# Second pass of the second MoE: activation steps of three blocks by turns, two sets of PSUM banks, stores from ScalarE's queue

## The chip, the cores and the metric

The program runs on one core of a Trainium2 chip. The metric is the device time of one execution in microseconds. A time given for a kernel is the median of several runs; a profile is one execution recorded by the hardware profiler, and its span runs from the first to the last instruction.

## What is computed

Three stages follow one another: a chunked attention, a first mixture of experts with a skip score, and a second stage that the reference calls MoE 2. Only the last one is touched. Its input is a matrix x of 4608 tokens by 512; `w_in` is 512 by 2048 and `w_out` 2048 by 512.

```python
def _moe2_ref(x, w_in, w_out):
    h = x @ w_in
    beta = 1.0
    neg = h <= -beta
    pos = h >= beta
    g = np.where(pos, h, np.where(neg, 0.0, (h + beta) ** 2 / (4.0 * beta)))
    return (g @ w_out).astype(np.float32)
```

## The kernel before, in words

The second stage cuts the 4608 tokens into 9 groups (`NG`) of 512 tokens (`GT`), and the 2048 hidden columns into 16 blocks (`NF`) of 128. A block (g, m) is a tile of 128 hidden columns by 512 tokens; there are 144 of them, in the order of the list `seq`. The stage runs in two passes over this list.

The first pass (`s_A`, L1147 and on) makes a block of h with 12 matmuls into a PSUM tile `a`, copies it on ScalarE to a tile `hs` (L1155) and stores it to a tensor `h_dram` from ScalarE's own queue (L1156).

The second pass reads each block back with `load_h` (L1158), a DMA of 256 KB from SyncE's queue into one of 8 buffers `hs` (`NH`). Then `s_G` computes the activation in six steps that take turns between ScalarE (ACT) and VectorE (DVE): Relu on ACT (L1167), maximum and subtraction on DVE (L1168), Square on ACT (L1169), the sum on DVE (L1170), the cast to the rounded half `gh` on ACT (L1171) and the remainder `gl` on DVE (L1172). Each step reads what the step before it wrote. The profile shows the tile that holds h as `hs`, the temporary as `r`, and `gh`, `gl` as `xh`, `xl` (they lie in the buffers `xh1`, `xl1`, four blocks deep, picked by `n % KD`). `w_out` is held as two halves too, `bh` and `bl` in the profile.

`s_B` multiplies the block: for each of the four token quarters t, three matmuls (gh by the high half, gh by the low half, gl by the high half) add to the PSUM tile `b0` to `b3`. So a block is 12 matmuls of 128 by 512, and the third one of the first quarter is the first that reads `gl`. At a group's last block (m = 15) each quarter's sum is copied out to a tile `o` (tag `s`, two buffers): t = 0 and 2 on ACT (L1188), 1 and 3 on DVE (L1186), and stored from SyncE's queue (L1190).

The order is written out by hand, and each engine follows its own instructions in the order of the program. In the loop at the end of `tile_attn_moe_kernel`, turn n runs `s_G` for block n, then `load_h` for block n + 6, then `s_B` for block n - 2 (`LAG` is 2).

Of the kernel before, what the change touches and what calls it, by code (L numbers as in the profile page):

```python
# [7 lines left out]
F32 = mybir.dt.float32  # L8
# [7 lines left out]
PSUM = bass.MemoryType.PSUM  # L16
# [3 lines left out]
NT, DM = B * S, H * D  # L20
NE, F1, F2 = 8, 1024, 2048
P = 128
CH = 64
KD = DM // P
# [9 lines left out]
NF = F2 // P  # L34
# [52 lines left out]
def kernel(ctx, tc, q, k, v, w_skip, w_gate, w1, w2, w_in, w_out, consts, out):  # L87
    nc = tc.nc
# [8 lines left out]
    dec_p = ctx.enter_context(tc.tile_pool(name="dec", bufs=2))  # L97
# [38 lines left out]
    def mm(o, l, r, start=True, stop=True):  # L136
        nc.tensor.matmul(out=o, lhsT=l, rhs=r, start=start, stop=stop)  # L137
# [80 lines left out]
    def settle():  # L218
        while done:
            next(done.pop(0), None)  # L220
# [72 lines left out]
    def warm(n, b=None):  # L293

        for _ in range(n):
            mm((big() if b is None else b)[:, 0:512], ones_b, cb[:, 0:512])
# [144 lines left out]
    def s_SEL(*us):  # L441

        if us[0] < 0:
            return []
        b = bank()
        for n, u in enumerate(us):
            ls = T.pop(("ls", u))
            for s in range(2):
                mm(b[:, 32 * n + 16 * s:32 * n + 16 * s + 16], ls[:, s * P:s * P + P], cst[:, 0:16])
        return e_SEL(us, b)  # L450
# [200 lines left out]
    xg_t, xt_t, h_t = {}, {}, {}  # L651
# [150 lines left out]
    with tc.manual_schedule():  # L802
# [44 lines left out]
        for i in range(NU - 1):  # L847
# [28 lines left out]
            a, r = s_SEL(i - 2), s_RANK(i - 3)  # L876
# [17 lines left out]
        b = s_SEL(u - 2)  # L894
# [19 lines left out]
        b = s_SEL(u - 1, u)  # L914
# [6 lines left out]
        w = s_RANK(u - 1, u)  # L921
# [17 lines left out]
        for s in range(4):  # L939
# [3 lines left out]
            out=key, in0=cnt, scalar=float(NE), in1=cst[:, C_PREF - C_SEL:C_PREF - C_SEL + NE], op0=ALU.mult, op1=ALU.add  # L943
# [7 lines left out]
            out=perm, in0=cst[r24, C_POS - C_SEL:C_POS - C_SEL + NL], scalar=own[r24, 1:2], in1=cst[r24, C_BLK - C_SEL:C_BLK - C_SEL + NL], op0=ALU.is_equal, op1=ALU.mult  # L951
# [42 lines left out]
    with tc.If(total > 0):  # L994
        fb = tc.tile_pool(name="fb", bufs=1, reuse_waits="tile")
        with fb as f_p, tc.For_i(0, NE, 1) as j:
# [4 lines left out]
            with tc.For_i(0, n_j, 1) as b:  # L1001
# [8 lines left out]
                    out=fx, out_offset=None, in_=x_dram[:, :], in_offset=bass.IndirectOffsetOnAxis(ap=fi[:, 0:1], axis=0)  # L1010
# [5 lines left out]
                for h in range(4):  # L1016
                    w = f_p.tile([P, KD, 2 * P], F32, tag="fw", name="fw", bufs=3)
                    nc.sync.dma_start(
                        out=w, in_=w1.rearrange("e (k p) f -> p (e k) f", p=P)[:, bass.ds(e * KD, KD), h * 2 * P:(h + 1) * 2 * P]
# [7 lines left out]
                for h in range(4):  # L1027
                    w = f_p.tile([P, 2, DM], F32, tag="fw", name="fw", bufs=3)
                    nc.sync.dma_start(
                        out=w, in_=w2.rearrange("e (f p) d -> p (e f) d", p=P)[:, bass.ds(e * (F1 // P) + 2 * h, 2), :]  # L1030
                    )
                    for a in range(2):
                        f = 2 * h + a
                        mm(bk, fh[:, f, :], w[:, a], f == 0, f == F1 // P - 1)
                nc.vector.scalar_tensor_tensor(
                    out=fx[:, 0:DM], in0=bk, scalar=fx[:, GATE:GATE + 1], in1=fx[:, 0:DM], op0=ALU.mult, op1=ALU.add
                )
                nc.gpsimd.indirect_dma_start(
                    out=x_dram[:, :],
                    out_offset=bass.IndirectOffsetOnAxis(ap=fi[:, 0:1], axis=0),  # L1040
                    in_=fx,
# [5 lines left out]
    xs_t, GT = {}, 512  # L1047
# [61 lines left out]


    ps_moe.close()
    p2 = ctx.enter_context(tc.tile_pool(name="p2", bufs=1, space=PSUM, reuse_waits="tile"))
    NG = NT // GT
    LAG = 2
    NH = 8
    x2_t, g_t, b_t, h_t = {}, [], {}, {}

    def t_X2(g, h, src, tag="t"):
        b = p2.tile([P, 512], F32, tag=tag, name=tag, bufs=2 if tag == "t" else 1)
        for kk in range(KD):  # L1120
            tr(b[:, kk * P:kk * P + P], src[:, kk * P:kk * P + P])
        return b

    def e_X2(g, h, a, b):
        if g not in x2_t:
            x2_t[g] = [x2_p.tile([P, KD, GT], F32R, tag=nm, name=nm, bufs=1) for nm in (f"xh{g % 2}", f"xl{g % 2}")]
        xh, xl = x2_t[g]
        b3 = b.rearrange("p (k n) -> p k n", k=KD)
        cut = slice((2 * h + a) * P, (2 * h + a + 1) * P)
        nc.scalar.copy(out=xh[:, :, cut], in_=b3)  # L1130
        nc.vector.tensor_tensor(out=xl[:, :, cut], in0=b3, in1=xh[:, :, cut], op=ALU.subtract)  # L1131

    def s_X2(g, h, tag="t"):
        bs = [t_X2(g, h, src, tag if tag == "t" else f"b{a}") for a, src in enumerate(xs_t.pop((g, h)))]
        return lambda: [e_X2(g, h, a, b) for a, b in enumerate(bs)]

    def mm_A(b, g, m, cut):
        xh, xl = x2_t[g]
        o = m % 8 * P
        for kk in range(KD):  # L1140
            wh, wl = (w[:, o:o + P] for w in w_t["in", kk * 2 + m // 8])
            for n, (w, x) in enumerate(((wh, xh), (wh, xl), (wl, xh))):
                mm(b[:, cut], w, x[:, kk, cut], kk == 0 and n == 0, kk == KD - 1 and n == 2)
# [14 lines left out]
    def load_h(g, m):  # L1158
        h_t[g, m] = g_p.tile([P, GT], F32, tag="hs", name="hs", bufs=NH)
        nc.sync.dma_start(out=h_t[g, m], in_=h_dram[g][m])  # L1160

    def s_G(n, g, m):

        h = h_t.pop((g, m))
        r = dec_p.tile([P, GT], F32, tag="a", name="r")
        gh, gl = (t[:, n % KD] for t in g_t)
        nc.scalar.activation(out=r, in_=h, func=ACTF.Relu, bias=bias[:, 0:1])  # L1167
        nc.vector.scalar_tensor_tensor(out=h, in0=h, scalar=-1.0, in1=r, op0=ALU.max, op1=ALU.subtract)  # L1168
        nc.scalar.activation(out=h, in_=h, func=ACTF.Square, scale=0.5, bias=bias[:, 1:2])  # L1169
        nc.vector.tensor_tensor(out=r, in0=r, in1=h, op=ALU.add)  # L1170
        nc.scalar.copy(out=gh, in_=r)  # L1171
        nc.vector.tensor_tensor(out=gl, in0=r, in1=gh, op=ALU.subtract)  # L1172

    def s_B(n, g, m):
        gh, gl = (t[:, n % KD] for t in g_t)
        wh, wl = (w[:, m % 2 * 512:m % 2 * 512 + 512] for w in w_t["out", m // 2])
        for t in range(4):
            if m == 0:
                b_t[t] = p2.tile([P, DM], F32, tag=f"b{t}", name=f"b{t}")
            cut = slice(t * P, t * P + P)  # L1180
            for n, (h, w) in enumerate(((gh, wh), (gh, wl), (gl, wh))):
                mm(b_t[t], h[:, cut], w, m == 0 and n == 0, m == NF - 1 and n == 2)
            if m == NF - 1:
                o = dec_p.tile([P, DM], F32, tag="s", name="o")
                if t % 2:
                    nc.vector.tensor_copy(o, b_t[t])  # L1186
                else:
                    nc.scalar.copy(out=o, in_=b_t[t])  # L1188
                r0 = g * GT + t * P
                nc.sync.dma_start(out=out[r0:r0 + P, :], in_=o)  # L1190

    a_t = {}
    with tc.manual_schedule():
        b = t_X2(0, 0, xs_t[0, 0][0])
        moe.close()
        x2_p = ctx.enter_context(tc.tile_pool(name="x2", bufs=2, reuse_waits="tile"))
        g_p = ctx.enter_context(tc.tile_pool(name="g", bufs=2, reuse_waits="tile"))
        e_X2(0, 0, 0, b)
        spare = p2.tile([P, DM], F32, tag="b3", name="spare")
        warm(8, spare)  # L1200
        e_X2(0, 0, 1, t_X2(0, 0, xs_t[0, 0][1]))
        warm(4, spare)
        load_x(0, 1)
        settle()
        for m in range(4):
            tag = "aatt"[m]
            a_t[0, m] = p2.tile([P, GT], F32, tag=tag, name=tag, bufs=2)
            if m == 3:
                rest = s_X2(0, 1, "b")
            mm_A(a_t[0, m], 0, m, slice(0, 2 * P))  # L1210
        rest()
        for m in range(4):
            mm_A(a_t[0, m], 0, m, slice(2 * P, GT))
        seq = [(g, m) for g in range(NG) for m in range(NF)]
        settle()
        for n, (g, m) in enumerate(seq):
            s_A(g, m)
            if n < KD:
                load_kept(KD + n)
            if n >= 8 and n % 6 == 0:  # L1220
                step()
            if n == len(seq) - 8:
                g_t.extend(x2_p.tile([P, KD, GT], F32R, tag=nm, name=nm, bufs=1) for nm in ("xh1", "xl1"))
            if n >= len(seq) - 8:
                load_h(*seq[n - len(seq) + 8])
            if n >= len(seq) - LAG:
                s_G(n - len(seq) + LAG, *seq[n - len(seq) + LAG])
            if g + 1 < NG:
                if m in (2, 6):
                    load_x(g + 1, m // 6)  # L1230
                if m in (8, 12):
                    s_X2(g + 1, m // 12)()
        settle()
        for n in range(LAG, len(seq) + LAG):
            if n < len(seq):
                s_G(n, *seq[n])
            if n + NH - 2 < len(seq):
                load_h(*seq[n + NH - 2])
            s_B(n - LAG, *seq[n - LAG])


# [22 lines left out]
```

## Time and profile before

| | us |
|---|---|
| median of 3 runs | 1481.36 (1478.95 to 1491.36) |
| the profiled execution's own time | 1479.77 |
| its span, first to last instruction | 1478.0 |

The profiled execution's time is 1.77 us longer than its span; sums over the trace are set against its own time, 1479.77, which is 1.6 us under the median. Over the span TensorE (PE) is busy 1329.7 us, VectorE 696.3, ScalarE 663.4 and GpSimd 214.1. A busy matmul here is counted to its modelled end and overlaps the next one, so PE's speed is read from the starts of its matmuls. The granted clock is a share: 1.00 is 2.4 GHz and 0.50 is 1.2 GHz. In the timeline a row gives the start, the duration, the engine, the line and operation, and in brackets how long the engine sat idle before it and what ended that.

### The profile page before, as it was taken

What the parts mean: (1) busy time and instruction counts of PE and PEld (TensorE: products, weight loads), DVE (VectorE), ACT (ScalarE), POOL (GpSimd) and SP (SyncE); (2) the same over time, 40 slices, a digit from 0 to 9 for tenths busy, and PEclk for the clock granted to TensorE, in tenths of its full rate; (3) what the DMA queues carried; (4) which work ended last, traced back from release to release, by engine and by line L of the source; (5) the groups of instructions that cost most, each with busy time, mean ns of one, the idle gap of its engine ahead of it and who ended that gap; (6) DMA issues with size and microseconds to landing.
All of it is one profiled execution on the core that took longest, in us unless ns stands there. A gap on an engine that the chain in (4) does not pass through costs nothing.

```text
span 1478.0 us, 19856 instructions
## 1 busy us (share of the span) xinstructions
PE 1329.7 (90%) x7127; PEld 1045.7 (71%) x7128; DVE 696.3 (47%) x1324; ACT 663.4 (45%) x1099; POOL 214.1 (14%) x259
## 2 busy tenths in 40 slices
PE   7867777899999899999999999889898898988987
PEld 6756666798799788888888888556555565565655
DVE  5644566477766911111112000455555555555554
ACT  7746653354443222223222222555555555555554
POOL 3011135333343610111111100000000000000000
PEclk9988897899999999999999999999999999999999
DMA  8888884577666653444333324323223223232231
GB/s 204 196 152 148 163 144 163 144 255 237 222 231 200 206 176 137 164 164 149 131 129 133 121 107 135 103 69 100 100 71 99 83 86 97 71 100 94 78 93 36
DMA packets 165372, 202.99 MB, mean 137 GB/s; under 512 B 51274, under 2 KB 88421, under 8 KB 165270
## 3 DMA queue, kind: packets, MB, share of 16 engines
q1 hardware_dynamic: 135862, 145.15, 36.2%
q10 hardware_dynamic: 21424, 37.83, 6.8%
q0 software_dynamic: 7984, 18.70, 3.9%
q8 instruction: 57, 0.93, 0.3%
q14 instruction: 45, 0.37, 0.1%
HBM read 135.88 MB, written 66.48 MB: 137 GB/s over the span
## 4 chain that ended last, share of the span: by engine, by line
PE 46%; ACT 17%; DVE 17%; issue 10%; DMA 8%; POOL 1%; ACTq 0%; another core or an unknown queue 0%; SPq 0%; DVEq 0%; POOLq 0%
PE a L137 26%; ACT hs L1169 7%; PE bank L137 7%; DVE r L1170 7%; DVE hs L1168 7%; ACT r L1167 7%; PE big L137 6%; PE big L140 5%; DMA stg<-in_moe_w_dram 1%; DMA out_dram<-o 1%; ACT xh L1171 1%; ACT qt L326 1%; PE t L140 1%; DMA m2w<-stg 1%; DMA stg<-in_moe_w_in_dram 1%
## 5 line engine op out<-in xcount | busy, mean ns | idle before, releaser
L137 PE MATMUL b<-bh,xh 128*128 128x512 f32 x576 | 246.5, 428 | 65.2 <-ACT o L1188 34.9
L137 PE MATMUL b<-bh,xl 128*128 128x512 f32 x576 | 242.6, 421 | 0.0
L137 PE MATMUL b<-bl,xh 128*128 128x512 f32 x576 | 231.3, 402 | 0.0
L137 PE MATMUL a<-xh,ah 128*128 128x512 f32 (+1 forms) x576 | 224.0, 389 | 0.0
L137 PE MATMUL a<-xl,ah 128*128 128x512 f32 (+1 forms) x576 | 222.6, 387 | 0.0
L137 PE MATMUL a<-xh,al 128*128 128x512 f32 (+1 forms) x576 | 222.6, 386 | 0.0
L137 PEld LDWEIGHTS b<-bh,xh 128*128 128x128 f32 x576 | 111.2, 193 | 137.1 <-ACT xh L1171 78.0
L1155 ACT COPY hs<-a 128x512 f32<-128x512 f32 x142 | 83.6, 589 | 276.1 <-PE a L137 265.5
L137 PEld LDWEIGHTS b<-bh,xl 128*128 128x128 f32 x576 | 111.1, 193 | 70.1 <-DVE xl L1172 49.5
L1169 ACT ACTIVATE hs<-hs,bias 128x512 f32<-128x512 f32 x144 | 104.2, 724 | 110.9 <-DVE hs L1168 110.9
L1170 DVE TENSOR_TENSOR r<-r,hs 128x512 f32<-128x512 f32 x144 | 99.7, 693 | 114.0 <-ACT hs L1169 114.0
L1172 DVE TENSOR_TENSOR xl<-r,xh 128x512 fp32r<-128x512 f32 x144 | 99.7, 693 | 106.5 <-ACT xh L1171 105.7
L1171 ACT CAST xh<-r 128x512 fp32r<-128x512 f32 x144 | 89.1, 619 | 117.2 <-DVE r L1170 115.0
L1131 DVE TENSOR_TENSOR xl<-t,xh 128x512 fp32r<-128x512 f32 x34 | 22.0, 687 | 231.4 <-ACT xh L1130 231.4
L137 PEld LDWEIGHTS b<-bl,xh 128*128 128x128 f32 x576 | 111.8, 194 | 19.4
L137 PEld LDWEIGHTS a<-xh,al 128*128 128x128 f32 x576 | 108.2, 188 | 22.0
L137 PEld LDWEIGHTS a<-xl,ah 128*128 128x128 f32 x576 | 108.2, 188 | 21.9 <-DVE xl L1131 0.5
L137 PEld LDWEIGHTS a<-xh,ah 128*128 128x128 f32 x576 | 108.2, 188 | 21.3
L1168 DVE SCALAR_TENSOR_TENSOR hs<-hs,r 128x512 f32<-128x512 f32 x144 | 99.6, 692 | 49.7 <-ACT r L1167 49.7
L1167 ACT ACTIVATE r<-hs,bias 128x512 f32<-128x512 f32 x144 | 103.8, 721 | 0.9 <-ACT hs L1155 0.9
L326 ACT COPY qt<-big 64x512 f32<-64x512 f32 x72 | 44.7, 621 | 64.2 <-PE big L140 56.6
L140 PE MATMUL big<-ident,qu 128*128 128x128 f32 x144 | 25.6, 335 | 47.6 <-issue 42.0
(217 smaller groups left out, 2041.4 us busy)
## 6 DMA issues: line engine op xcount, KB each, us to landing
h_dram<-hs ACTq DMA_DIRECT2D x144, 256.0 KB
hs<-h_dram SPq DMA_DIRECT2D x144, 256.0 KB
stg<-in_moe_w_dram SPq DMA_DIRECT2D x128, 256.0 KB
vbd<-in_v_dram SPq DMA_DIRECT2D x144, 64.0 KB
out_dram<-o SPq DMA_DIRECT2D x36, 256.0 KB
xs<-x_dram SPq DMA_DIRECT2D x17, 512.0 KB
x_dram<-xn SPq DMA_DIRECT2D x16, 516.0 KB
stg<-in_moe_w_in_dram SPq DMA_DIRECT2D x16, 512.0 KB
```

Of the source, the lines that this page charges most:

```text
L137: nc.tensor.matmul(out=o, lhsT=l, rhs=r, start=start, stop=stop)
L140: nc.tensor.transpose(out=o, in_=i, identity=ident)
L326: (nc.vector.tensor_copy if eng is nc.vector else nc.scalar.copy)(out=o, in_=b4[64 * r:64 * r + 64, :, par, :])
L1131: nc.vector.tensor_tensor(out=xl[:, :, cut], in0=b3, in1=xh[:, :, cut], op=ALU.subtract)
L1155: nc.scalar.copy(out=hs, in_=b)
L1167: nc.scalar.activation(out=r, in_=h, func=ACTF.Relu, bias=bias[:, 0:1])
L1168: nc.vector.scalar_tensor_tensor(out=h, in0=h, scalar=-1.0, in1=r, op0=ALU.max, op1=ALU.subtract)
L1169: nc.scalar.activation(out=h, in_=h, func=ACTF.Square, scale=0.5, bias=bias[:, 1:2])
L1170: nc.vector.tensor_tensor(out=r, in0=r, in1=h, op=ALU.add)
L1171: nc.scalar.copy(out=gh, in_=r)
L1172: nc.vector.tensor_tensor(out=gl, in0=r, in1=gh, op=ALU.subtract)
```

## The change

`s_G` is cut into `G1` (Relu and the DVE step behind it), `G2` (Square and the sum) and `G3` (the cast and the remainder). Turn k now runs `G3` for block k - 2, `G2` for block k - 1 and `G1` for block k. `LAG` becomes 3, so `load_h` runs 5 blocks ahead of the turn. The temporary `r` alternates between the tags `a` and `s`, two buffers each. Ahead of the second pass the pool `p2` is closed, and a pool `p3` gives each of `b0` to `b3` two buffers, that is all eight PSUM banks. The four sums of a group go to one tile `o` of four quarters (in the place of `xh0`). In every group but the last all four are copied on ACT and stored from ACT's queue; in the last group quarters 1 and 3 are copied on DVE and stored from SyncE's queue.

```diff
-    LAG = 2
+    LAG = 3
-    def s_G(n, g, m):
-
-        h = h_t.pop((g, m))
-        r = dec_p.tile([P, GT], F32, tag="a", name="r")
-        gh, gl = (t[:, n % KD] for t in g_t)
+    def G1(n):
+
+        h = h_t[seq[n]]
+        r = r_t[n] = dec_p.tile([P, GT], F32, tag="as"[n % 2], name="r")
         nc.scalar.activation(out=r, in_=h, func=ACTF.Relu, bias=bias[:, 0:1])
         nc.vector.scalar_tensor_tensor(out=h, in0=h, scalar=-1.0, in1=r, op0=ALU.max, op1=ALU.subtract)
+
+    def G2(n):
+        h, r = h_t.pop(seq[n]), r_t[n]
         nc.scalar.activation(out=h, in_=h, func=ACTF.Square, scale=0.5, bias=bias[:, 1:2])
         nc.vector.tensor_tensor(out=r, in0=r, in1=h, op=ALU.add)
+
+    def G3(n):
+        r = r_t.pop(n)
+        gh, gl = (t[:, n % KD] for t in g_t)
         nc.scalar.copy(out=gh, in_=r)
         nc.vector.tensor_tensor(out=gl, in0=r, in1=gh, op=ALU.subtract)
+    def s_G(k):
+        for d, f in ((2, G3), (1, G2), (0, G1)):
+            if 0 <= k - d < len(seq):
+                f(k - d)
...
-                b_t[t] = p2.tile([P, DM], F32, tag=f"b{t}", name=f"b{t}")
+                b_t[t] = p3.tile([P, DM], F32, tag=f"b{t}", name=f"b{t}", bufs=2)
...
-                o = dec_p.tile([P, DM], F32, tag="s", name="o")
-                if t % 2:
+                o = o_t[0][:, t]
+                r0 = g * GT + t * P
+                if g == NG - 1 and t % 2:
                     nc.vector.tensor_copy(o, b_t[t])
+                    nc.sync.dma_start(out=out[r0:r0 + P, :], in_=o)
                 else:
                     nc.scalar.copy(out=o, in_=b_t[t])
-                r0 = g * GT + t * P
-                nc.sync.dma_start(out=out[r0:r0 + P, :], in_=o)
+                    nc.scalar.dma_start(out=out[r0:r0 + P, :], in_=o)
...
         settle()
+        second.close()
+        o_t.append(x2_p.tile([P, 4, DM], F32, tag="xh0", name="o", bufs=1))
+        p3 = ctx.enter_context(tc.tile_pool(name="p3", bufs=1, space=PSUM, reuse_waits="tile"))
         for n in range(LAG, len(seq) + LAG):
-            if n < len(seq):
-                s_G(n, *seq[n])
-            if n + NH - 2 < len(seq):
-                load_h(*seq[n + NH - 2])
-            s_B(n - LAG, *seq[n - LAG])
+            s_G(n)
+            if n + NH - LAG < len(seq):
+                load_h(*seq[n + NH - LAG])
+            s_B(n - LAG)
```

On ScalarE, a few blocks into the second pass, before the change (the tiles carry their numbers: `r_9148` and `hs_9035` belong to one block, and each wait is on an engine's or a DMA's semaphore):

```order
L1167 ACTIVATE r_9148<-hs_9035,bias_85 128x512 [waits DMAHW2_49,Activation_49]
L1169 ACTIVATE hs_9035<-hs_9035,bias_85 128x512 [waits DVE_49]
L1171 CAST xh1_8979<-r_9148 128x512 [waits DVE_49]
L1167 ACTIVATE r_9169<-hs_9053,bias_85 128x512 [waits DMAHW4_49,Activation_49]
L1169 ACTIVATE hs_9053<-hs_9053,bias_85 128x512 [waits DVE_49]
L1171 CAST xh1_8979<-r_9169 128x512 [waits DVE_49,PE_49]
```

The same place after the change, with three blocks in each turn (`r_9121`, then `hs_9035`, then `r_9158`):

```order
L1179 CAST xh1_8979<-r_9121 128x512 [waits DVE_49]
L1173 ACTIVATE hs_9035<-hs_9035,bias_85 128x512 [waits DVE_49]
L1168 ACTIVATE r_9158<-hs_9053,bias_85 128x512 [waits DMAHW4_49,Activation_49]
L1179 CAST xh1_8979<-r_9133 128x512 [waits DVE_49]
L1173 ACTIVATE hs_9053<-hs_9053,bias_85 128x512 [waits DVE_49]
L1168 ACTIVATE r_9179<-hs_9071,bias_85 128x512 [waits DMAHW6_49,Activation_49]
```

Before, three neighbouring rows are one block and each reads what DVE made from the row above it; now the row above a step belongs to another block.

On ScalarE at the end of the first group, before the change (`b0_9132` and `b2_9140` are the group's sums):

```order
L1167 ACTIVATE r_9442<-hs_9323,bias_85 128x512 [waits DMAHW5_49,Activation_49]
L1169 ACTIVATE hs_9323<-hs_9323,bias_85 128x512 [waits DVE_49]
L1171 CAST xh1_8979<-r_9442 128x512 [waits DVE_49,PE_49]
L1188 COPY o_9454<-b0_9132 128x512 [waits PE_49]
L1188 COPY o_9466<-b2_9140 128x512 [waits DMAHW4_49,PE_49,Activation_49]
L1167 ACTIVATE r_9475<-hs_9344,bias_85 128x512 [waits DMAHW6_49]
L1169 ACTIVATE hs_9344<-hs_9344,bias_85 128x512 [waits DVE_49]
```

The same place after the change:

```order
L1179 CAST xh1_8979<-r_9410 128x512 [waits DVE_49,PE_49]
L1173 ACTIVATE hs_9329<-hs_9329,bias_85 128x512 [waits DVE_49]
L1168 ACTIVATE r_9452<-hs_9350,bias_85 128x512 [waits DMAHW6_49,Activation_49]
L1204 COPY o_9125<-b0_9138 128x512 [waits PE_49]
L1205 DMA out_0_dram<-o_9125 128x512 [waits Activation_49]
L1204 COPY o_9125<-b1_9142 128x512 [waits PE_49]
L1205 DMA out_0_dram<-o_9125 128x512 [waits DMAHW7_49,Activation_49]
L1204 COPY o_9125<-b2_9146 128x512 [waits PE_49]
L1205 DMA out_0_dram<-o_9125 128x512 [waits DMAHW0_49,Activation_49]
L1204 COPY o_9125<-b3_9150 128x512 [waits PE_49]
L1205 DMA out_0_dram<-o_9125 128x512 [waits DMAHW1_49,Activation_49]
L1179 CAST xh1_8979<-r_9431 128x512 [waits DVE_49]
```

Four copies and four store issues now stand between two turns, where two copies stood; the cast of the next block but one (`r_9431`) stands behind them.

On TensorE at the start of the second group (`b0_9484` to `b2_9492` are the new group's sums), before the change:

```order
L137 MATMUL b0_9484<-bh0_6562,xh1_8979 128x512 [waits Activation_49]
L137 MATMUL b0_9484<-bl0_6563,xh1_8979 128x512
L137 MATMUL b0_9484<-bh0_6562,xl1_8980 128x512 [waits DVE_49]
L137 MATMUL b1_9488<-bh0_6562,xh1_8979 128x512 [waits DVE_49]
L137 MATMUL b1_9488<-bl0_6563,xh1_8979 128x512
L137 MATMUL b1_9488<-bh0_6562,xl1_8980 128x512
L137 MATMUL b2_9492<-bh0_6562,xh1_8979 128x512 [waits Activation_49]
```

And after it:

```order
L137 MATMUL b0_9486<-bh0_6562,xh1_8979 128x512 [waits Activation_49]
L137 MATMUL b0_9486<-bl0_6563,xh1_8979 128x512
L137 MATMUL b0_9486<-bh0_6562,xl1_8980 128x512 [waits DVE_49]
L137 MATMUL b1_9490<-bh0_6562,xh1_8979 128x512
L137 MATMUL b1_9490<-bl0_6563,xh1_8979 128x512
L137 MATMUL b1_9490<-bh0_6562,xl1_8980 128x512
L137 MATMUL b2_9494<-bh0_6562,xh1_8979 128x512
```

The waits of the second and third quarter for the copies out of their banks are gone; the waits of the first and third matmul for `gh` and `gl` stay.

## Rows read from the trace of the kernel before

**Rows 1.** Groups by line, 975 to 1470 us: count, busy us, mean ns, idle before, releasers.
```profile
L137 PE MATMUL b<-bh,xh 128*128 128x512 f32 x528 | 226.3, 429 | 59.2 <-ACT o L1188 34.9 <-ACT xh L1171 24.2
...
L1169 ACT ACTIVATE hs<-hs,bias 128x512 f32<-128x512 f32 x132 | 95.6, 724 | 101.8 <-DVE hs L1168 101.8
```

**Rows 2.** Timeline of ACT and of DVE over one block, start and duration in us.
```profile
1101.11 0.62 ACT L1171 CAST xh<-r 128x512 fp32r<-128x512 f32 x1 [0.82 <-DVE r L1170]
1101.64 0.72 ACT L1167 ACTIVATE r<-hs,bias 128x512 f32<-128x512 f32 x1
1103.12 0.72 ACT L1169 ACTIVATE hs<-hs,bias 128x512 f32<-128x512 f32 x1 [0.76 <-DVE hs L1168]
1104.66 0.62 ACT L1171 CAST xh<-r 128x512 fp32r<-128x512 f32 x1 [0.81 <-DVE r L1170]
...
1101.76 0.69 DVE L1172 TENSOR_TENSOR xl<-r,xh 128x512 fp32r<-128x512 f32 x1 [0.74 <-ACT xh L1171]
1102.39 0.69 DVE L1168 SCALAR_TENSOR_TENSOR hs<-hs,r 128x512 f32<-128x512 f32 x1
1103.88 0.69 DVE L1170 TENSOR_TENSOR r<-r,hs 128x512 f32<-128x512 f32 x1 [0.79 <-ACT hs L1169]
```

**Rows 3.** Timeline of PE in the same block.
```profile
1101.79 0.50 PE L137 MATMUL b<-bh,xh 128*128 128x512 f32 x1 [0.26 <-ACT xh L1171]
...
1102.51 0.50 PE L137 MATMUL b<-bh,xl 128*128 128x512 f32 x1
1102.85 0.40 PE L137 MATMUL b<-bh,xh 128*128 128x512 f32 x1
...
1104.70 0.40 PE L137 MATMUL b<-bh,xl 128*128 128x512 f32 x1
```

**Rows 4.** Busy time (instructions) of PE, PEld, DVE, ACT, POOL; PEclk, DMA share, GB/s.
```profile
800.00:900.00 100.00, 100.00 (x459) 83.15 (x458) 7.51 (x12) 27.26 (x47) 7.74 (x6) 1.00 0.31 110
```

**Rows 5.** Timeline of PE in the second pass, where blocks were waiting for it.
```profile
1121.08 0.39 PE L137 MATMUL b<-bh,xl 128*128 128x512 f32 x1
...
1126.97 0.39 PE L137 MATMUL b<-bl,xh 128*128 128x512 f32 x1
```

**Rows 6.** Timeline of PE and ACT at the change from the first pass to the second.
```profile
931.55 0.39 PE L137 MATMUL a<-xh,al 128*128 128x512 f32 x1
...
933.86 0.58 ACT L1155 COPY hs<-a 128x512 f32<-128x512 f32 x1
...
934.00 0.50 PE L137 MATMUL b<-bh,xh 128*128 128x512 f32 x1 [2.07 <-ACT xh L1171]
...
934.90 0.72 ACT L1167 ACTIVATE r<-hs,bias 128x512 f32<-128x512 f32 x1 [0.46 <-ACT hs L1155]
```

**Rows 7.** Timeline of ACT and PE at the end of a group.
```profile
1115.80 0.58 ACT L1188 COPY o<-b 128x512 f32<-128x512 f32 x1
...
1116.43 0.50 PE L137 MATMUL b<-bh,xh 128*128 128x512 f32 x1 [4.27 <-ACT o L1188]
...
1118.54 0.59 ACT L1188 COPY o<-b 128x512 f32<-128x512 f32 x1 [2.16 <-DMA out_dram<-o]
```

**Rows 8.** Stretches of 2 us before and after that group's end, columns as in Rows 4.
```profile
1108.00:1110.00 2.00, 1.76 (x7) 0.85 (x6) 1.26 (x3) 1.24 (x2) 0.00 (x0) 1.00 0.42 87
...
1116.00:1118.00 2.00, 1.57 (x5) 1.11 (x6) 1.22 (x2) 0.38 (x1) 0.00 (x0) 0.79 0.34 131
1118.00:1120.00 2.00, 1.74 (x5) 0.92 (x4) 0.62 (x2) 1.21 (x2) 0.00 (x0) 0.50 0.35 134
1120.00:1122.00 2.00, 2.00 (x9) 1.57 (x9) 1.21 (x3) 0.72 (x1) 0.00 (x0) 0.86 0.75 280
```

**Rows 9.** Timeline of the end, and the stores (duration ns min/median/max, first and last start).
```profile
1470.08 0.50 PE L137 MATMUL b<-bh,xl 128*128 128x512 f32 x1
...
1470.62 0.59 ACT L1188 COPY o<-b 128x512 f32<-128x512 f32 x1 [1.32 <-PE b L137]
...
1474.14 0.69 DVE L1186 COPY o<-b 128x512 f32<-128x512 f32 x1 [2.13 <-DMA out_dram<-o]
...
L1190 SPq DMA_DIRECT2D out_dram<-o x36: 332/335/338, 995.9 to 1474.9; - x36
```

More of the change, by code (lines that the diff above doesn't have):

```diff
@@ L1111 @@
     ps_moe.close()
-    p2 = ctx.enter_context(tc.tile_pool(name="p2", bufs=1, space=PSUM, reuse_waits="tile"))
+    second = ExitStack()
+    p2 = second.enter_context(tc.tile_pool(name="p2", bufs=1, space=PSUM, reuse_waits="tile"))
     NG = NT // GT
-    LAG = 2
+    LAG = 3
     NH = 8
-    x2_t, g_t, b_t, h_t = {}, [], {}, {}
+    x2_t, g_t, o_t, b_t, h_t, r_t = {}, [], [], {}, {}, {}
+    seq = [(g, m) for g in range(NG) for m in range(NF)]
     def t_X2(g, h, src, tag="t"):
@@ L1160, in load_h, with s_B @@
         nc.sync.dma_start(out=h_t[g, m], in_=h_dram[g][m])
-    def s_G(n, g, m):
-        h = h_t.pop((g, m))
-        r = dec_p.tile([P, GT], F32, tag="a", name="r")
-        gh, gl = (t[:, n % KD] for t in g_t)
+    def G1(n):
+        h = h_t[seq[n]]
+        r = r_t[n] = dec_p.tile([P, GT], F32, tag="as"[n % 2], name="r")
         nc.scalar.activation(out=r, in_=h, func=ACTF.Relu, bias=bias[:, 0:1])
         nc.vector.scalar_tensor_tensor(out=h, in0=h, scalar=-1.0, in1=r, op0=ALU.max, op1=ALU.subtract)
+    def G2(n):
+        h, r = h_t.pop(seq[n]), r_t[n]
         nc.scalar.activation(out=h, in_=h, func=ACTF.Square, scale=0.5, bias=bias[:, 1:2])
         nc.vector.tensor_tensor(out=r, in0=r, in1=h, op=ALU.add)
+    def G3(n):
+        r = r_t.pop(n)
+        gh, gl = (t[:, n % KD] for t in g_t)
         nc.scalar.copy(out=gh, in_=r)
         nc.vector.tensor_tensor(out=gl, in0=r, in1=gh, op=ALU.subtract)
-    def s_B(n, g, m):
+    def s_G(k):
+        for d, f in ((2, G3), (1, G2), (0, G1)):
+            if 0 <= k - d < len(seq):
+                f(k - d)
+    def s_B(n):
+        g, m = seq[n]
         gh, gl = (t[:, n % KD] for t in g_t)
@@ L1178, in s_B @@
             if m == 0:
-                b_t[t] = p2.tile([P, DM], F32, tag=f"b{t}", name=f"b{t}")
+                b_t[t] = p3.tile([P, DM], F32, tag=f"b{t}", name=f"b{t}", bufs=2)
             cut = slice(t * P, t * P + P)
-            for n, (h, w) in enumerate(((gh, wh), (gh, wl), (gl, wh))):
-                mm(b_t[t], h[:, cut], w, m == 0 and n == 0, m == NF - 1 and n == 2)
+            for i, (h, w) in enumerate(((gh, wh), (gh, wl), (gl, wh))):
+                mm(b_t[t], h[:, cut], w, m == 0 and i == 0, m == NF - 1 and i == 2)
             if m == NF - 1:
-                o = dec_p.tile([P, DM], F32, tag="s", name="o")
-                if t % 2:
+                o = o_t[0][:, t]
+                r0 = g * GT + t * P
+                if g == NG - 1 and t % 2:
                     nc.vector.tensor_copy(o, b_t[t])
+                    nc.sync.dma_start(out=out[r0:r0 + P, :], in_=o)
                 else:
                     nc.scalar.copy(out=o, in_=b_t[t])
-                r0 = g * GT + t * P
-                nc.sync.dma_start(out=out[r0:r0 + P, :], in_=o)
+                    nc.scalar.dma_start(out=out[r0:r0 + P, :], in_=o)
     a_t = {}
@@ L1213 @@
             mm_A(a_t[0, m], 0, m, slice(2 * P, GT))
-        seq = [(g, m) for g in range(NG) for m in range(NF)]
         settle()
@@ L1221 @@
                 step()
-            if n == len(seq) - 8:
+            if n == len(seq) - NH:
                 g_t.extend(x2_p.tile([P, KD, GT], F32R, tag=nm, name=nm, bufs=1) for nm in ("xh1", "xl1"))
-            if n >= len(seq) - 8:
-                load_h(*seq[n - len(seq) + 8])
+            if n >= len(seq) - NH:
+                load_h(*seq[n - len(seq) + NH])
             if n >= len(seq) - LAG:
-                s_G(n - len(seq) + LAG, *seq[n - len(seq) + LAG])
+                s_G(n - len(seq) + LAG)
             if g + 1 < NG:
```

## The prediction, made before the changed kernel ran

> **What bounds the kernel now.** I read the groups by line over the second pass first, then the timeline of one block, then the stretches with the granted clock, and last the two ends of the pass. The groups show who waits: Square on ACT is busy 95.6 us and idle before it 101.8 us, always for DVE's step, and PE's first matmul of a block is idle 59.2 us, always for ACT [rows 1]. So neither elementwise engine is full, and PE waits for both. The timeline of a block shows why. Starts follow each other so: Relu 1101.64, DVE's step 1102.39, Square 1103.12, DVE's sum 1103.88, cast 1104.66 [rows 2]. Those are gaps of 0.75, 0.73, 0.76 and 0.78 us, and from a cast to the next Relu it is 0.53 (1101.11 to 1101.64). Their sum is 3.55 us, which is the distance from one cast to the next. This chain of five links, each waiting for the other engine, is the period of a block; only the remainder step lies beside it.
>
> PE needs less. Where finished blocks wait for it, its matmuls start at 1121.08 and 1126.97 with 25 others between [rows 5], that is 26 steps in 5.89 us, 0.2267 us each, and 12 of them are 2.72 us. In the block above it stalls twice: 0.26 us idle before its first matmul, and from the first to the third 0.72 us where two steps would be 0.45 [rows 3]. At a group's end it waits once more, 4.27 us for the copy of the sums [rows 7], because that copy stands on ACT behind a whole chain and the banks of the next group are the same banks.
>
> **The change part by part.** *The turns.* Nothing is added: three instructions on ACT and three on DVE a block, as before. What goes is that neighbours depend on each other. The shortest loop is now Square of block k-1, Relu of block k behind it on ACT, DVE's step on k, Square of k: the last two links are 0.75 and 0.73 us [rows 2]. The first link, an ACT instruction directly behind a Square, is not shown before. Its bounds are 0.53 us (a Relu directly behind a cast of 0.62) and 0.72 us, a Square to its end with no overlap [rows 2]. I take 0.63, the Square's 0.72 less the 0.09 by which the cast is overlapped. That gives 2.11 us a block, between 2.01 and 2.20. DVE alone needs three starts 0.63 us apart (1101.76 to 1102.39), 1.89 us. All of it is under PE's 2.72 us, so either end costs nothing, and PE becomes the bound of a block. The Trainium skill, page "ScalarE: Activation LUTs", section "What ACT_TABLE_LOAD costs", says that ACTIVATEs back to back overlap by about 93 ns; by it the link would be 0.63 us, the loop the same 2.11. The overlap behind a cast agrees (0.62 less 0.53 [rows 2]).
>
> *PE.* 144 blocks of 12 matmuls are 1728 steps. At 0.2267 us they take 391.7 us. As a check that PE holds this at length with the full clock: 100 us of the first pass have PE busy throughout at 1.00 [rows 4]. The other end is the pace behind a stall, 8 steps from 1102.85 to 1104.70, 0.231 us each [rows 3], which would be 399.6 us. A matmul of this shape cannot be counted faster than 0.2267, since it is already the pace where nothing makes it wait. I take 0.2267, because the stalls behind which the slower pace stood go.
>
> *The start.* PE's last matmul of the first pass starts at 931.55 and ends at 931.94 [rows 6]. Today ACT copies its result only at 933.86, after a whole chain. Now Square and Relu of early blocks are done beside PE's work, so the copy can start at about 931.97. A copy with the issue of its store takes ACT 1.04 us (933.86 to 934.90 [rows 6]). The first cast then starts at 933.01, and PE follows a cast by 0.68 us (1101.11 to 1101.79 [rows 2, 3]): first matmul at 933.7, against 934.00 now. Its `gl` comes 1.40 us behind the cast's start (1101.11 to 1102.51) where the third matmul is ready 1.13 behind it, so 0.3 us are lost, and about 0.1 more on picking up again (0.34 to the next start instead of 0.23 [rows 3]): 0.4 in all.
>
> *A group's end.* Two sets of banks take away the wait for copies, and four quarters of `o` the wait for earlier stores (2.16 us [rows 7]). What is late next is the cast that stands behind the copies on ACT. Let the group's last block start on PE at T. The first quarter's third matmul starts at T + 0.45; ACT's copy follows such a start by 0.5 us (1470.08 to 1470.62 [rows 9]), so it starts at T + 0.9 to 1.0. Four copies with their stores are 4 x 1.04 = 4.16 us and end at T + 5.1. PE has one finished block in hand, so it wants the next cast's block at T + 5.44. It gets it at 5.1 + 0.68 = 5.78, and `gl` with a further loss as at the start: 0.3 to 0.35, plus 0.3. I take 0.65 us at each of 8 group ends, 5.2 us. The bounds are nothing (copies that follow the quarters without the wait for a store's issue end before PE asks) and what a group's end takes now, 4.27 us of idleness. ACT then gains 2.72 - 2.11 = 0.6 us a block on PE and is ahead again long before the next end. Queued behind a store's issue on ACT is only this; the issue's own waits are for loads of blocks that were issued two turns or more before.
>
> *Loads.* SyncE's queue now holds loads alone, except for two stores at the very end. A load takes its buffer 8 blocks behind its last reader, and is read 7 turns later, 15 us or more. A block is 256 KB in 2.72 us, 94 GB/s, and with the stores 118; 280 GB/s were moved at a time [rows 8]. I cost them at nothing; what hides them is the 15 us.
>
> *The end.* The pass ends its last step at 933.7 + 0.4 + 391.7 + 5.2 = 1331.0. The last sum is copied on DVE 0.3 us later (0.5 behind the last start). Today the last copy waits 2.13 us for a store [rows 9]; now it has its own quarter. Its store is issued 0.76 us behind the copy's start (1474.14 to 1474.9), and from there the span ends 3.1 us later (1478.0). So 1331.3 + 0.8 + 3.1 = 1335.2. With the 1.8 us around the span the time is 1337 us, 143 under the profiled execution's 1479.77, which is 1.6 under the median.
>
> **The rivals.** *The clock falls.* After PE's 4.27 us of idleness the clock is granted at 0.79, 0.50 and 0.86 in three stretches of 2 us [rows 8], so 2 x (0.21 + 0.50 + 0.14) = 1.7 us of work are lost. If the short stalls at the group ends did the same, 8 x 1.7 = 14 us come on top: 1351 us. Against it: two stalls in every block, 0.26 and 0.27 us, leave the clock at 1.00 (2.4 GHz) [rows 3, 8]. The Trainium skill, page "TensorE: Matmul & The Clock Gate", section "A second HAM failure mode: psum-queue depth-cycling", reports a kernel that cycled through PSUM banks and idled briefly between groups of matmuls, whose clock went up and down. By that rule the eight banks would bring this rival; the rows of one block do not show it.
>
> *A group's end stays as it is.* If four stores issued from ACT hold its queue as long as the chain did, each of 8 ends costs 4.27 + 1.7 us instead of 0.65: 43 us more, 1380 us. For it speaks that the copies still stand ahead of a cast [rows 7]; against it, that a whole block of 2.72 us is in hand.
>
> *The engines take turns.* If a step is let go only when the other engine has finished its whole turn, three steps run on one, then three on the other: 0.53 + 0.63 + 0.75 on ACT and 0.63 + 0.63 + 0.73 on DVE up to the next cast, 3.90 us a block [rows 2]. The copies then have no cover, 4.16 us at 8 ends: 933.7 + 144 x 3.90 + 33 + 4 + 2 = 1534 us, slower than before. It decides from about 3.5 us a block. Against it: today each step is let go 0.04 to 0.07 us behind the one it needs, though nothing shows a wait with more work queued behind the releaser.
>
> *The chain stays 3.55.* If the order written does not make the engines overlap, the time stays near 1480. The waits that each step has left speak against it.
>
> **How the numbers follow.** PE as the bound with small ends: 0.85. The clock: 0.06. Ends as now: 0.05. Turns: 0.03. No effect: 0.01. The likeliest gives 1337; with no stall at group ends it is 1332, with the slower pace 1345, and the clock's rival 1351 with that pace 1359. The range is 1329 to 1357. Faster by over 1% (about what a measurement of this kernel can tell from no change) has 0.96, within 1% 0.01, slower 0.03.
>
> **What would show it.** Right: in the second pass PE starts a block each 2.72 us with the clock at 1.00, ACT and DVE each busy some 2 us of it, Square and the sum hardly idle for the other engine, PE idle under 1 us at a group's end, first matmul near 933.7. Wrong: casts more than 2.72 us apart within a group, a granted clock under 1.00 behind group ends, PE idle for ACT by several us there, or a load named as the releaser of Relu.

## The result, and the profile after

| | before | changed |
|---|---|---|
| median, us | 1483.24 (4 runs, 1478.95 to 1491.36) | 1339.28 (4 runs, 1335.77 to 1345.91) |
| profiled execution's own time, us | 1479.77 | 1335.77 |
| its span, us | 1478.0 | 1334.0 |

The ratio is 0.903, with a 95% interval of 0.897 to 0.908: faster, by some 144 us. The forecast was 1337 us, in a range of 1329 to 1357.

The two traces put 142.2 of the 144.0 us between the spans into the second pass. From the starts of PE's matmuls:

| us | before | changed | difference |
|---|---|---|---|
| last matmul of the first pass starts | 931.55 | 931.72 | +0.17 |
| from there to the first of the second pass | 2.45 | 2.08 | -0.37 |
| from that one to the last (1728 matmuls) | 538.25 | 396.08 | -142.17 |
| from that one to the end of the span | 5.75 | 4.12 | -1.63 |

The groups by line of the changed kernel, 940 to 1330 us, answer to [rows 1]:

```profile
L137 PE MATMUL b<-bh,xh 128*128 128x512 f32 x568 | 221.9, 391 | 0.0
...
L1173 ACT ACTIVATE hs<-hs,bias 128x512 f32<-128x512 f32 x140 | 101.3, 724 | 0.0
...
L1179 ACT CAST xh<-r 128x512 fp32r<-128x512 f32 x141 | 87.8, 622 | 50.8 <-PE b L137 32.5 <-DVE r L1174 12.6 <-ACT o L1204 3.3
```

Square no longer waits for DVE (0.0 where it was 101.8), PE's first matmuls show no idleness (what PE still loses is shorter than the modelled overlap of its matmuls and is read from their starts, below), and the cast now waits most for PE: it finds its buffer still being read. The bound has changed sides. The stretches of 40 us (columns as in [rows 4]) say the same: PE is busy throughout, at the full clock.

```profile
1020.00:1060.00 40.00, 40.00 (x176) 32.52 (x175) 31.12 (x48) 32.65 (x52) 0.00 (x0) 1.00 0.46 125
1060.00:1100.00 40.00, 40.00 (x176) 32.51 (x175) 28.11 (x44) 29.92 (x48) 0.00 (x0) 1.00 0.46 123
```

The timeline of ACT and DVE over one turn behind a group's end, where ACT is catching up, answers to [rows 2]:

```profile
1070.03 0.62 ACT L1179 CAST xh<-r 128x512 fp32r<-128x512 f32 x1
1070.64 0.73 ACT L1173 ACTIVATE hs<-hs,bias 128x512 f32<-128x512 f32 x1
1071.27 0.71 ACT L1168 ACTIVATE r<-hs,bias 128x512 f32<-128x512 f32 x1
1072.12 0.62 ACT L1179 CAST xh<-r 128x512 fp32r<-128x512 f32 x1
...
1070.68 0.69 DVE L1180 TENSOR_TENSOR xl<-r,xh 128x512 fp32r<-128x512 f32 x1
1071.40 0.69 DVE L1174 TENSOR_TENSOR r<-r,hs 128x512 f32<-128x512 f32 x1
1072.01 0.69 DVE L1169 SCALAR_TENSOR_TENSOR hs<-hs,r 128x512 f32<-128x512 f32 x1
```

Both engines run without a bracket of idleness, ACT three steps and DVE three steps side by side, and from cast to cast it is 2.09 us where it was 3.55. The link that had to be guessed, a Relu directly behind a Square, is 0.63 us (1070.64 to 1071.27).

### The profile page after: what moved, and what is told of

It is laid out like the page before. It is cut to its first block, busy times and chain, and to the rows that moved or that the text cites. A ratio compares the mean times of both kernels' runs of the same rounds, so it can differ in the third digit from the quotient of the medians.

```text
span 1334.0 us, 19838 instructions
## 1 busy us (share of the span) xinstructions
PE 1243.2 (93%) x7127; PEld 1049.1 (79%) x7128; DVE 682.8 (51%) x1308; ACT 663.4 (50%) x1115; POOL 214.5 (16%) x259
## 4 chain that ended last, share of the span: by engine, by line
PE 79%; DVE 5%; DMA 5%; issue 5%; ACT 3%; POOL 2%; SPq 0%; ACTq 0%; POOLq 0%; DVEq 0%
PE b L137 30%; PE a L137 29%; PE bank L137 7%; PE big L137 6%; PE big L140 5%; DMA stg<-in_moe_w_dram 2%; PE t L140 1%; ACT qt L326 1%; DMA idx_dram<-cst,si 1%; DVE a L192 1%; DVE acc L555 1%; DVE a L191 1%; DMA ku<-in_k_dram 1%; DMA stg<-in_moe_w_in_dram 0%; POOL idx_dram L578 0%
## 5 line engine op out<-in xcount | busy, mean ns | idle before, releaser
L137 PE MATMUL b<-bh,xh 128*128 128x512 f32 x576 | 225.2, 391 | 1.7 <-ACT xh L1179 1.7
L137 PE MATMUL b<-bh,xl 128*128 128x512 f32 x576 | 225.1, 391 | 0.0
L137 PE MATMUL b<-bl,xh 128*128 128x512 f32 x576 | 224.2, 389 | 0.0
L137 PEld LDWEIGHTS b<-bh,xh 128*128 128x128 f32 x576 | 108.1, 188 | 26.9 <-ACT xh L1179 5.1
L137 PEld LDWEIGHTS b<-bh,xl 128*128 128x128 f32 x576 | 108.1, 188 | 26.0 <-DVE xl L1180 3.9
L137 PEld LDWEIGHTS b<-bl,xh 128*128 128x128 f32 x576 | 108.1, 188 | 22.3
```

## The experiments

Executions differ by up to 15 us in what lies ahead of the second pass (the last matmul of the first pass starts between 916.8 and 931.9 us in the traces below). So kernels that ran once are compared by their second pass, from its first matmul's start to its last one's. The changed kernel's is 396.08 us.

**The turns undone.**

```diff
-    LAG = 3
+    LAG = 2
-        for d, f in ((2, G3), (1, G2), (0, G1)):
+        for d, f in ((0, G1), (0, G2), (0, G3)):
```

> The turns alone are undone: a turn runs all six steps of one block and LAG is 2 again; the two sets of banks, the four quarters of o and the stores from ACT's queue stay. Theory (the turns carry the whole gain): casts are 3.55 us apart again, and since ACT is now the bound its four copies with stores, 4.16 us, come on top at each of 8 group ends: second pass 144 x 3.55 + 33 = 544 us, span near 1485 us, no better than the kernel before. Rival (banks, stores and o carry a share of their own): the 4.27 us of PE idleness at a group's end go and nothing takes their place, second pass some 516 us, span near 1455 us.

Measured: second pass 541.97 us, span 1471.4. Casts are 3.54 us apart. The kernel before, run beside it on the same chip, took 1469.5 us, this one 1473.2. The groups by line, 960 to 1460 us, show the waits of [rows 1] again:

```profile
L137 PE MATMUL b<-bh,xh 128*128 128x512 f32 x530 | 227.1, 429 | 59.7 <-ACT xh L1179 59.7
...
L1173 ACT ACTIVATE hs<-hs,bias 128x512 f32<-128x512 f32 x133 | 96.2, 724 | 101.0 <-DVE hs L1169 101.0
```

PE's waits at group ends are now all put down to the cast, not to a copy: with two sets of banks the copy no longer holds PE, but the cast behind four copies does, for just as long (4.6 us between starts, as before the change). Without the turns the other parts are worth nothing. The edit takes `LAG` back together with the turns, and `LAG` 3 with one block in a turn was not run; the experiment with two blocks, below, keeps `LAG` 3, and its time still follows the chain that its turns leave.

**One set of banks.**

```diff
-                b_t[t] = p3.tile([P, DM], F32, tag=f"b{t}", name=f"b{t}", bufs=2)
+                b_t[t] = p3.tile([P, DM], F32, tag=f"b{t}", name=f"b{t}")
```

> The changed kernel with one buffer for each of the four sums instead of two. Theory: in the changed kernel's trace each copy ends 0.3 us or more before PE comes back to that bank (copy of the fourth quarter 1067.02 to 1067.61, PE there at 1067.91), so nothing waits: second pass 396 us as in the changed kernel, within 1 us, span 1334 to 1335. Rival (the second set is what lets PE go on at a group's end): PE waits for copies again, 1 us or more at each of 8 ends, second pass 404 us or more.

Measured: second pass 397.58 us, 1.5 more. The group ends are as in the changed kernel, four steps of 0.33 to 0.39 us each. Timeline at an end, the fourth quarter's copy and PE's return to its bank:

```profile
1016.70 0.59 ACT L1204 COPY o<-b 128x512 f32<-128x512 f32 x1 [0.41 <-ACT o L1204]
...
1017.59 0.39 PE L137 MATMUL b<-bh,xh 128*128 128x512 f32 x1
```

The copy has ended at 1017.29 when PE comes at 1017.59. The 1.5 us lie at the pass's start, in the clock (columns as in [rows 4]):

```profile
926.00:928.00 2.00, 2.00 (x6) 1.39 (x7) 1.93 (x4) 1.85 (x4) 0.00 (x0) 0.82 0.68 223
928.00:930.00 2.00, 2.00 (x6) 1.52 (x6) 1.91 (x3) 1.79 (x3) 0.00 (x0) 0.50 0.83 262
```

Eight steps there are 0.43 us long instead of 0.23, 1.6 us in all. Such steps stand in four other traces below, with both sets of banks too, so they are not the edit's. The second set of banks is worth nothing in the changed kernel.

**Stores from SyncE's queue.**

```diff
-                    nc.scalar.dma_start(out=out[r0:r0 + P, :], in_=o)
+                    nc.sync.dma_start(out=out[r0:r0 + P, :], in_=o)
```

> The changed kernel with the stores of the sums issued from SyncE's queue, the copies still on ACT. Theory (the 0.5 us that PE loses at a group's end is the wait for a cast behind four copies with store issues): without the issues a copy takes what PE's quarter takes, 0.68 us, the next cast starts about 1.3 us earlier and PE loses nothing: second pass 392 us, span 1330. Rival (stores in SyncE's queue hold up the loads behind them): Relu waits for a load, casts late after each group's end, second pass above 396 us.

Measured: second pass 393.48 us, with eight steps at half the clock at its start; without them it would be 391.9. No step at any group end is longer than 0.25 us. Timeline at one end, ACT alone (four copies in one row):

```profile
1012.65 2.63 ACT L1204 COPY o<-b 128x512 f32<-128x512 f32 x4 [4.49 <-PE b L137]
1015.17 0.63 ACT L1179 CAST xh<-r 128x512 fp32r<-128x512 f32 x1
```

The cast starts 2.52 us behind the first copy, against 3.99 in the changed kernel (1064.03 to 1068.02). No load is late. Of the edits at a group's end, issuing the stores from ACT is the one that costs time. That ACT makes four copies instead of two costs PE nothing here; two of them given back to DVE were not run.

**LAG 4.**

```diff
-    LAG = 3
+    LAG = 4
```

> The changed kernel with LAG 4: PE has two finished blocks in hand instead of one. Theory: the cast behind the copies is wanted 2.72 us later, so the 0.5 us at 8 group ends go; and the first cast is made before the last block of the first pass, so PE starts the second pass within 0.3 us of the first one's end (931.95 to 932.2 instead of 933.80): second pass 391.6 us, span near 1327.8, about 6 us less. Rival (the stalls belong to something else than the cast, the change of banks for one): 0.5 us stays at each end, and the start waits for the last copy out of PSUM: span 1332 to 1334.

Measured: second pass 391.45 us, which is 1727 steps of 0.2267 with none longer than 0.25; span 1317.3. Timeline at the change of passes, then the stretch from 930 to 1300 us:

```profile
921.47 0.39 PE L137 MATMUL a<-xh,al 128*128 128x512 f32 x1
921.70 0.39 PE L137 MATMUL b<-bh,xh 128*128 128x512 f32 x1
```

```profile
930.00:1300.00 370.00, 370.00 (x1634) 306.35 (x1633) 269.08 (x414) 278.03 (x446) 0.00 (x0) 1.00 0.38 117
```

PE goes from one pass to the other without a pause: 0.23 us from start to start, where the changed kernel has 2.08. The four stores still go out from ACT, so the 0.5 us at a group's end were indeed the lateness of the cast, and of the remainder behind it, and not the change of banks, which this kernel makes too.

**Two buffers for the copied sums.**

```diff
-                o = o_t[0][:, t]
+                o = o_t[t % 2]
...
-        o_t.append(x2_p.tile([P, 4, DM], F32, tag="xh0", name="o", bufs=1))
+        oo = x2_p.tile([P, 4, DM], F32, tag="xh0", name="o", bufs=1)
+        o_t.extend(oo[:, a] for a in range(2))
```

> The changed kernel with two buffers for the copied sums instead of four. Theory: the third copy waits until the first store has landed, some 2 us behind its issue, the fourth for the second: the cast behind them comes about 0.7 us later, PE loses 1.2 us instead of 0.5 at each of 8 group ends: second pass 402 us, span near 1340. Rival (a store lands before its buffer is wanted again, as copies with issues take 1 us each): nothing changes, 396 us.

Measured: second pass 403.49 us, 1.6 of them eight steps at half the clock at the start, so 401.9. The first wait of a group's end is 1.08 us between starts instead of 0.33. Timeline of ACT there:

```profile
1019.37 0.59 ACT L1204 COPY o<-b 128x512 f32<-128x512 f32 x1 [1.09 <-DMA out_dram<-o]
...
1020.42 0.59 ACT L1204 COPY o<-b 128x512 f32<-128x512 f32 x1 [0.47 <-DMA out_dram<-o]
```

The third copy waits for the first store, and the span's end comes 5.59 us behind the last matmul's start instead of 4.12, for the same reason.

**Two blocks by turns.**

```diff
-        for d, f in ((2, G3), (1, G2), (0, G1)):
+        for d, f in ((0, G1), (1, G2), (1, G3)):
```

> The turns hold two blocks instead of three: Relu with its DVE step for block k, then Square, sum, cast and remainder of block k - 1; LAG stays 3. By the links of the trace a turn's loop is Relu to Square 0.63, Square to sum 0.76, sum to cast 0.78, cast to the next Relu 0.52: 2.69 us, a hair under PE's 2.72. Theory: within a group casts are 2.7 us apart and ACT cannot make up the 4.16 us of copies at a group's end: 16 x 2.69 + 4.16 = 47.2 us a group, second pass near 421 us, span near 1359. Rivals: two blocks are enough and PE stays the bound, 396 us; or two blocks wait as one did, 3.55 us a block, 511 us or more.

Measured: second pass 420.22 us, span 1357.8. Casts within a group are 2.67 to 2.68 us apart. Timeline of ACT over one turn:

```profile
1001.83 0.62 ACT L1179 CAST xh<-r 128x512 fp32r<-128x512 f32 x1 [0.81 <-DVE r L1174]
1002.36 0.72 ACT L1168 ACTIVATE r<-hs,bias 128x512 f32<-128x512 f32 x1
1002.98 0.71 ACT L1173 ACTIVATE hs<-hs,bias 128x512 f32<-128x512 f32 x1
1004.51 0.62 ACT L1179 CAST xh<-r 128x512 fp32r<-128x512 f32 x1 [0.81 <-DVE r L1174]
```

Each cast waits 0.81 us for the sum of its own block. The period is just under PE's 2.72, so in the 16 blocks of a group ACT gains only 0.8 us on PE, and the rest of what four copies cost is paid at each end. From one end to the next it is 46.7 us on average, which is 16 x 2.67 + 4.0. The third block in the turns buys the slack that covers the copies.

**PE lightened.** This kernel leaves out one of the three products.

```diff
-            for i, (h, w) in enumerate(((gh, wh), (gh, wl), (gl, wh))):
-                mm(b_t[t], h[:, cut], w, m == 0 and i == 0, m == NF - 1 and i == 2)
+            for i, (h, w) in enumerate(((gh, wh), (gl, wh))):
+                mm(b_t[t], h[:, cut], w, m == 0 and i == 0, m == NF - 1 and i == 1)
```

> The changed kernel with two matmuls a quarter instead of three (the product of the rounded half with the low half of the weights is left out), so that PE needs 8 x 0.2267 = 1.81 us a block. It measures what ACT and DVE can do by turns. Theory: casts 2.11 us apart (2.01 to 2.20), and with four copies of about 1.0 us a group takes 16 x 2.11 + 4.1 = 37.9 us: second pass near 341 us, span near 1279. Rival (the turns cost more than the links say and PE hides it): casts 2.4 us apart or more, second pass 380 us or more.

Measured: second pass 331.5 us, span 1256.5. Timeline of ACT, with one row of DVE:

```profile
1006.81 0.62 ACT L1179 CAST xh<-r 128x512 fp32r<-128x512 f32 x1 [0.20 <-DVE r L1174]
1007.37 0.72 ACT L1173 ACTIVATE hs<-hs,bias 128x512 f32<-128x512 f32 x1
1008.00 0.71 ACT L1168 ACTIVATE r<-hs,bias 128x512 f32<-128x512 f32 x1
1008.91 0.62 ACT L1179 CAST xh<-r 128x512 fp32r<-128x512 f32 x1 [0.20 <-DVE r L1174]
1009.47 0.72 ACT L1173 ACTIVATE hs<-hs,bias 128x512 f32<-128x512 f32 x1
...
1008.74 0.69 DVE L1169 SCALAR_TENSOR_TENSOR hs<-hs,r 128x512 f32<-128x512 f32 x1
```

Casts are 2.10 us apart, turn after turn, and a group takes 37.2 us. The loop that the prediction named is there link by link: Square of one block 1007.37, Relu of the next 1008.00, DVE's step on it 1008.74, its Square 1009.47, that is 0.63, 0.74 and 0.73 us. A second loop, from Square to the sum that DVE makes of it (1008.12) and to the step behind the sum, adds up to the same 2.10, and this trace does not tell the two apart. The expectation of 341 counted the copies at nine ends; eight hold up PE, and 8 x 37.9 + 16 x 2.11 is 337. What was measured, 8 x 37.2 + 16 x 2.10 = 331, has the same form.

**LAG 4 and stores from SyncE's queue,** both edits as above.

> Both at once: LAG 4 and the stores from SyncE's queue. Theory: each alone takes the 0.5 us from the group ends, so together they give what LAG 4 gives: second pass 391.6 us, span near 1327.8, about 6 us less than the changed kernel; 0.4% is at the edge of what five rounds tell. Rival (the loads are held up by stores that wait for their copies): longer than with LAG 4 alone by several us.

Measured: second pass 391.45 us, the same as with LAG 4 alone, which ran on another chip. The median of 6 runs is 1325.1 us (1314.6 to 1328.8) against 1471.6 of the kernel before on the same chip: ratio 0.900, interval 0.897 to 0.903. Nothing is gained over LAG 4 alone and nothing is held up.

**The changed kernel and LAG 4 side by side,** on one chip, edits as above.

> The changed kernel itself, beside LAG 4 on the same chip. Every theory expects the second pass to take 396 us, or 398 if the clock falls once at its start, where PE pauses 1.7 us.

> LAG 4 on the same chip as the changed kernel beside it. Theory: second pass 391.5 us with no step longer than 0.25 us, first matmul within 0.3 us of the last of the first pass; 6.5 us less than the changed kernel, 0.5%, more where the changed kernel's clock falls. Rival (what the second pass gains is lost in the parts ahead of it, which differ by up to 15 us from run to run): no difference in the median.

Measured: the changed kernel 1327.96 us (5 runs, 1326.7 to 1332.9), ratio to the kernel before 0.902, interval 0.9006 to 0.9039. LAG 4 1323.64 us (6 runs, 1314.3 to 1325.7), ratio 0.899, interval 0.8979 to 0.9003. In their traces the second pass is 397.60 and 391.45 us, and the pause ahead of it 2.10 and 0.23. That is 8.0 us; the medians differ by 4.3, and the parts ahead of the pass vary by more than this. Each of the six runs of LAG 4 is shorter than each of the five of the changed kernel, and the intervals of the two ratios do not meet, though only just: LAG 4 is the faster of the two, by some 0.3%.

## Why the prediction was right

*The bound of a block.* Forecast: chain 3.55 us before, loop of 2.11 (2.01 to 2.20) after, PE at 2.72 as the bound. Shown: with one block in a turn 3.54, with two 2.67, with three 2.10 where PE asks for less. The links read from one block of the trace of before, with the guessed 0.63 us between Square and Relu, gave all three periods within 0.02 us (2.69 for two blocks, in the expectation of that experiment).

*PE's pace.* Forecast 0.2267 us a step, 391.7 for the pass. LAG 4 shows it without any stall: 391.45 from first to last start. The slower pace of 0.231 stands only behind stalls, as argued. (The 459 matmuls in 100 us of [rows 4] look faster, 0.218 each, because short ones of 128 by 128 are among them; those of 128 by 512 start 0.227 us apart there too.)

*The start.* Forecast 933.7, with 0.4 us lost behind it. Measured 933.80 (the first pass ended 0.17 later in this execution). Timeline of the changed kernel, answering to [rows 6]:

```profile
931.72 0.39 PE L137 MATMUL a<-xh,al 128*128 128x512 f32 x1
...
932.15 0.59 ACT L1157 COPY hs<-a 128x512 f32<-128x512 f32 x1 [0.38 <-PE a L137]
...
933.13 0.62 ACT L1179 CAST xh<-r 128x512 fp32r<-128x512 f32 x1 [0.40 <-ACT hs L1157]
...
933.80 0.50 PE L137 MATMUL b<-bh,xh 128*128 128x512 f32 x1 [1.69 <-ACT xh L1179]
```

Copy, cast and first matmul follow as the steps said.

*A group's end.* Forecast 0.65 us, measured 0.5. The timeline answers to [rows 7]; the group's last block starts at T = 1063.15:

```profile
1063.15 0.39 PE L137 MATMUL b<-bh,xh 128*128 128x512 f32 x1
...
1064.03 0.59 ACT L1204 COPY o<-b 128x512 f32<-128x512 f32 x1 [4.49 <-PE b L137]
...
1067.02 0.59 ACT L1204 COPY o<-b 128x512 f32<-128x512 f32 x1 [0.41 <-ACT o L1204]
...
1068.02 0.62 ACT L1179 CAST xh<-r 128x512 fp32r<-128x512 f32 x1 [0.41 <-ACT o L1204]
1068.36 0.39 PE L137 MATMUL b<-bh,xl 128*128 128x512 f32 x1
...
1068.69 0.50 PE L137 MATMUL b<-bh,xh 128*128 128x512 f32 x1
...
1069.42 0.50 PE L137 MATMUL b<-bh,xl 128*128 128x512 f32 x1
1069.76 0.40 PE L137 MATMUL b<-bh,xh 128*128 128x512 f32 x1
```

The cast starts at T + 4.87, not T + 5.1: the first copy came at T + 0.88, and a copy with its store's issue is 1.00 us (1067.02 to 1068.02), not 1.04. The four steps from 1068.36 to 1069.76 take 1.40 us instead of 0.91, and that is the 0.5. Only 0.1 of it lies ahead of the block's first matmul, where the cast counts (forecast about 0.34); 0.4 lies in the three steps around `gl` (forecast 0.3). So the sum came near by a cast that was less late and a remainder that cost a little more. Eight ends cost 4 us instead of 5.2. That this term begins with the late cast is shown twice, by LAG 4 and by the stores from SyncE's queue; each alone takes it away.

*Where a reason was wrong though its term was small.* "Two sets of banks take away the wait for copies": they do when the turns are undone, and the wait then goes to the cast. In the changed kernel one set would do. PE's 4.27 us at a group's end came from ACT being late with its copies by more than a whole chain. The third matmul of the first quarter starts at 1109.60, and the copy of that quarter at 1115.80 [rows 7], 6.2 us later:

```profile
1109.60 0.50 PE L137 MATMUL b<-bh,xl 128*128 128x512 f32 x1
```

Once ACT is ahead, the copy follows that matmul by 0.43 us (0.88 us into the last block), and the banks are free before PE returns. The four quarters of `o`, on the other hand, are worth 0.75 us at each end, as two buffers showed.

*Loads.* Forecast at nothing: no Relu waits for a load in the changed kernel's second pass, and 125 and 123 GB/s were moved in the two stretches above (forecast 118).

*The end.* The last matmul starts at 1329.88, the last copy on DVE at 1330.31, its store is issued at 1331.0, and the span ends at 1334.0; forecast 0.5, 0.8 and 3.1 us, measured 0.43, 0.7 and 3.0:

```profile
1329.88 0.39 PE L137 MATMUL b<-bh,xl 128*128 128x512 f32 x1
...
1330.31 0.69 DVE L1201 COPY o<-b 128x512 f32<-128x512 f32 x1 [0.67 <-PE b L137]
...
L1202 SPq DMA_DIRECT2D out_dram<-o x2: 338/338/338, 1329.7 to 1331.0; - x2
```

*The rivals.* The engines do not wait for each other's whole turn: 2.10 us, not 3.90. Group ends do not stay as they were. The clock did not fall at group ends, in any trace with ends of 0.5 us; in the changed kernel it stays at 1.00 from 940 to 1330 us with eight banks in use. The Trainium skill, page "TensorE: Matmul & The Clock Gate", section "A second HAM failure mode: psum-queue depth-cycling", reports a kernel whose clock swung as PE went through the banks with short idle times; this trace does not show that. But the rival was real in another place, below.

*What was luck.* The median, 1339.28 us, lies 2 us from the forecast, while what lies ahead of the second pass differs by up to 15 us from one execution to another; on another chip the same kernel took 1327.96, with the same ratio of 0.90. The second pass is the fairer test: 0.4 + 391.7 + 5.2 = 397.3 us were forecast, and 396.3 were measured with the last step counted in, or 397.8 in the execution whose clock fell. The forecast has no term for that fall.

## What to carry to other kernels

When two engines hand one tile to and fro, add up the start-to-start links of the chain from one block of the trace, then write down the loops that are left if each engine's neighbours belong to different blocks: the longest of these loops, not the engines' busy time, says how many blocks have to be in a turn. Take one block more than the period needs if something else (copies, stores) visits the engine now and then, for the slack is what hides it. An engine that feeds the bound should have enough finished work in hand to cover its longest visit elsewhere; here a second finished block (LAG 4) took both the stalls at group ends and the pause between the passes.

## What the runs showed that was not expected

The same pause makes the clock fall in one execution and not in another. Ahead of the second pass PE's starts lie 2.07 to 2.10 us apart in six traces (1.7 us idle). In the changed kernel's first trace the clock stayed at 1.00 (2.4 GHz). In the other five (one set of banks, stores from SyncE's queue, two buffers for the sums, PE lightened, the changed kernel again) seven or eight of the following steps take 0.43 us, at 0.50 (1.2 GHz), which costs up to 1.6 us. At the eight group ends of the trace with two blocks by turns, pauses of 2.89 to 3.21 us between starts were followed by a clock of 0.50 in four cases of five, and pauses of 1.37 to 1.94 in none of three. A pause of 2.45 us in the trace of before left the clock alone too, and one of 2.46 with the turns undone did not. The argument that short stalls leave the clock at 1.00 rested on stalls of 0.26 us and does not reach to 1.7. LAG 4 has no such pause, and none of its traces shows a slow step.
